# Output projection of two block pairs as seven products of sums in an attention and gated feed-forward kernel

## The chip, the cores and the metric

The kernel runs on one core of one Trainium2 chip. The metric is the device time of one execution in microseconds (us). The engines named below are TensorE (PE in the profile; its weight loads are PEld), VectorE (DVE), ScalarE (ACT), GpSimd (POOL) and SyncE (SP, which issues nearly all DMAs). TensorE, VectorE and ScalarE each carry out their instructions in the order in which the code emits them.

## The reference

Attention inside chunks of 64 positions, then a gated feed-forward layer over all tokens, in float32:

```
q_c, k_c, v_c: (8, 8, 9, 64, 64)        # batch, head, chunk, position, depth
attn = softmax(q_c @ k_c^T / 8)          # 64 x 64 per chunk and head
x = (attn @ v_c), as 4608 tokens x 512
g = x @ w_gate                           # 512 -> 1536
h = silu(g) * (x @ w_val)
out = h @ w_out                          # 1536 -> 512
```

## The kernel before

The 4608 tokens are nine blocks (`NB`) of 512 tokens (`N`); a block has four tiles (`T`) of 128 tokens. The 1536 inner columns are twelve steps (`NF`) of 128. Float32 accuracy comes from splitting each operand into a rounded high part and a low part (`split`, L60 to L63: a copy on ScalarE, a subtraction on VectorE) and adding three matmuls, low by high, high by low, high by high. Every matmul has its own weight load.

Blocks 0 to 2 run first. Blocks 3 to 8 run as three pairs, (3, 4), (5, 6) and (7, 8), here called pair 3, 5 and 7, in the loop at L1306. For a pair the gate and value products of both blocks come from seven products in place of eight (a scheme of Strassen's kind): `gated_pair` (L1152) calls `seventh` seven times per step, each six matmuls of 128x512 into PSUM (L883), and copies, adds and multiplies the results on ScalarE and VectorE (L1165 to L1189, `add` at L887, `times` at L522). Products 0, 2, 4 and 6 add up in one bank `ps1`, which is read between them. Its result is `h` for the first block and `h2` for the second.

The output projection is then done block by block. `project` (L537) multiplies the split `h` of one step (`hh`, `hl`, from `parts`, L529) by 512 columns of `w_out`, four tiles by three matmuls of 128x512 (L552 to L554), into the four banks of `ps_o`. For the first block of a pair this happens one step late inside `gated_pair`: `turn_of(t)` puts tile t's three matmuls between the products of the next step. The second block's `h2` is kept in SBUF (`both_steps`, L1200), and `second_steps` (L1211) projects it afterwards, twelve steps of twelve matmuls. The weights of a step, `both`, are fetched by `out_again` (L494) and the factors of the seven products by `load_weights` (L1144), both on SP's queue.

Beside a pair's steps run the scores, softmax and turned columns of the next pair's attention: `bursts` are short runs of small matmuls at the end of a step, `middle` and `behind` hold ScalarE and VectorE work, of which `turn_some` issues four 32x32 block transposes for each of its parts (L355). In pair 3 and pair 5 the sums and splits of the next pair's input (`x0`, `s1`, `x1`, `s4`, `s2`, `x2` to `x6`, L1104 to L1139) are made one per step of `second_steps`, from the list `later` (L1318). Step 11 of the last pair splits `h` ahead of its last product (`ending`, L1175), and the last tile of the last block is done in two column halves (L545 to L575).

PSUM has eight banks: two `ps_a`, two `ps_gv`, four `ps_o`. SBUF buffers are reused by tags, among them `moved(i)`, one of twelve large buffers.

## Time and profile before

| what | value |
|---|---|
| median of 3 runs | 891.84 us (891.74 to 892.16) |
| the profiled execution | 892.38 us |
| its span | 890.6 us |
| steps of pair 5, gated part | 515.57 to 671.50 us |
| second block of pair 5 | 671.5 to 704.3 us |
| steps of pair 7, gated part | 704.3 to 851.2 us |
| VectorE busy over the span | 547.6 us |
| ScalarE busy over the span | 389.0 us |
| DMA, mean | 251 GB/s |

Everything in the profile belongs to one execution, whose time is in the second line; its span is the part in which instructions ran. A row of the timeline gives the start and the duration in us, the engine, the line of the kernel, the operation, and output <- input with their shapes; in brackets stands how long the engine had been idle and what released it. A row of the groups ends in the total busy time, the mean of one in ns, and the idle time ahead. A row of the windows gives a stretch of the span, its length, the busy time of PE, PEld, DVE, ACT and POOL in it, the granted clock, and the DMA's share and GB/s. Matmuls are pipelined: the distance between two starts is what one costs, not its listed duration.

### The profile page before, as it was taken

To read this page: it belongs to the slowest core of one execution; us is meant where nothing else is said; L and a number is where in the kernel's file an instruction comes from. 1 tells how busy PE (TensorE), PEld (TensorE's weight loads), DVE (VectorE), ACT (ScalarE), POOL (GpSimd) and SP (SyncE) were. 2 spreads that over 40 slices of the span, in tenths; PEclk is the share of its full clock that TensorE was granted. 3 is DMA by queue.
4 is the path that set the end of the run, shared out by engine and by line. 5 is a ranking of instruction groups with operands and counts; after the bars stand their busy time and mean duration, and the time that the engine had idled before them with its cause. 6 is when DMAs were issued, how large, how long until landed. Compare 5 with 4: busy or idle time off the path is not lost.

```text
span 890.6 us, 14742 instructions
## 1 busy us (share of the span) xinstructions
PE 880.2 (99%) x6034; PEld 729.3 (82%) x6034; DVE 547.6 (61%) x831; ACT 389.0 (44%) x594; POOL 39.7 (4%) x32
## 2 busy tenths in 40 slices
PE   7999999999999999999999999999999999999998
PEld 6788888888888888888888888888888888888886
DVE  6888999673888656776753656767645433333332
ACT  5757777544442345225325444244325432223232
POOL 1100000000055110000000000000000000000000
PEclk9999999999999999999999999999999999999999
DMA  9767778889799777657577867566657475555651
GB/s 357 266 253 297 262 286 320 336 284 348 222 392 279 277 254 238 248 215 255 207 250 291 299 208 268 194 236 245 199 213 278 177 272 203 198 196 230 237 189 47
DMA packets 73314, 223.25 MB, mean 251 GB/s; under 512 B 30752, under 2 KB 31264, under 8 KB 59040
## 3 DMA queue, kind: packets, MB, share of 16 engines
q1 hardware_dynamic: 71664, 219.57, 67.7%
q10 hardware_dynamic: 1584, 2.75, 0.9%
q8 instruction: 47, 0.77, 0.3%
q14 instruction: 19, 0.16, 0.1%
HBM read 178.78 MB, written 43.52 MB: 250 GB/s over the span
## 4 chain that ended last, share of the span: by engine, by line
PE 94%; DVE 3%; DMA 1%; issue 1%; ACT 0%; SPq 0%; ACTq 0%; DVEq 0%
PE ps_a L883 26%; PE ps_gv L883 19%; PE ps_gv L478 12%; PE ps_o L552 11%; PE ps_o L553 11%; PE ps_o L554 11%; PE ps_a L290 2%; DMA qk_t<-in_qk 1%; PE ps_a L368 1%; PE ps_a L468 0%; DVE both L677 0%; DVE t L90 0%; DVE th L165 0%; DVE w L130 0%; DVE h L522 0%
## 5 line engine op out<-in xcount | busy, mean ns | idle before, releaser
L883 PE MATMUL ps_a<-x,factors 128*128 128x512 f32 x864 | 219.2, 389 | 0.0
L883 PEld LDWEIGHTS ps_a<-x,factors 128*128 128x128 f32 x864 | 162.2, 188 | 33.7
L883 PE MATMUL ps_gv<-x,factors 128*128 128x512 f32 x648 | 164.4, 389 | 0.0
L883 PEld LDWEIGHTS ps_gv<-x,factors 128*128 128x128 f32 x648 | 121.6, 188 | 25.3
L552 PE MATMUL ps_o<-both,hl 128*128 128x512 f32 x336 | 131.8, 392 | 0.0
L553 PE MATMUL ps_o<-both,hh 128*128 128x512 f32 x336 | 130.7, 389 | 0.0
L554 PE MATMUL ps_o<-both,hh 128*128 128x512 f32 x336 | 130.6, 389 | 0.0
L63 DVE TENSOR_TENSOR hl<-h,hh 128x512 fp32r<-128x512 f32 x98 | 68.2, 696 | 65.0 <-ACT hh L62 64.8
L62 ACT CAST hh<-h 128x512 fp32r<-128x512 f32 x98 | 60.5, 617 | 95.7 <-PE ps_o L554 51.3
L478 PE MATMUL ps_gv<-xh,w 128*128 128x512 f32 x320 | 97.9, 391 | 0.2 <-ACT xh L638 0.2
L887 DVE TENSOR_TENSOR h<-h,ps_gv 128x512 f32<-128x512 f32 x44 | 30.2, 686 | 103.9 <-PE ps_gv L883 103.7
L355 DVE STREAM_TRANSPOSE turned<-s_sb 32x256 f32<-32x256 f32 x192 | 83.7, 436 | 2.7
L522 DVE SCALAR_TENSOR_TENSOR h<-v,h 128x512 f32<-128x512 f32 x88 | 60.9, 692 | 38.0 <-ACT h L1188 33.3
L552 PEld LDWEIGHTS ps_o<-both,hl 128*128 128x128 f32 x336 | 63.0, 188 | 13.5
L554 PEld LDWEIGHTS ps_o<-both,hh 128*128 128x128 f32 x336 | 63.1, 188 | 13.2
L553 PEld LDWEIGHTS ps_o<-both,hh 128*128 128x128 f32 x336 | 63.1, 188 | 12.7
L1188 ACT ACTIVATE h<-ps_a 128x512 f32<-128x512 f32 x36 | 21.5, 598 | 112.2 <-PE ps_a L883 112.2
L478 PEld LDWEIGHTS ps_gv<-xh,w 128*128 128x128 f32 x320 | 59.8, 188 | 12.9 <-ACT xh L638 0.5
L478 PE MATMUL ps_gv<-xl,w 128*128 128x512 f32 x160 | 61.3, 393 | 0.0
L887 DVE TENSOR_TENSOR v<-v,ps_a 128x512 f32<-128x512 f32 x44 | 30.2, 687 | 41.1 <-PE ps_a L883 36.4
L1174 ACT ACTIVATE h<-h 128x512 f32<-128x512 f32 x36 | 22.8, 632 | 53.0 <-DVE h L887 52.9
L887 DVE TENSOR_TENSOR v<-v,ps_gv 128x512 f32<-128x512 f32 x44 | 30.2, 687 | 24.3 <-PE ps_gv L883 24.2
(143 smaller groups left out, 1069.0 us busy)
## 6 DMA issues: line engine op xcount, KB each, us to landing
factors<-w SPq DMA_DIRECT2D x36, 1024.0 KB, 4.8
factors<-t SPq DMA_DIRECT2D x36, 1024.0 KB, 6.0
both<-o SPq DMA_DIRECT2D x70, 512.0 KB, 6.4
w<-w SPq DMA_DIRECT2D x16, 1024.0 KB, 7.9
t<-th SPq DMA_DIRECT2D x24, 512.0 KB, 4.2
two<-o SPq DMA_DIRECT2D x12, 1024.0 KB, 5.2
raw<-in_wgv SPq DMA_DIRECT2D x11, 1024.0 KB, 8.6
qk_t<-in_qk SPq DMA_DIRECT2D x10, 1024.0 KB, 7.8
```

Source lines behind the costliest of these rows:

```text
L62: nc.scalar.copy(out=hi, in_=src)
L63: (engine or nc.vector).tensor_tensor(out=lo, in0=src, in1=hi.bitcast(F32), op=ALU.subtract)
L355: nc.vector.transpose(out=self.turned[to:to + 32, p:p + 2, j, :, 32 * (i % 2):32 * (i % 2) + 32], in_=src[32 * i:32 * i + 32, :, o // 2, 3 ...
L478: nc.tensor.matmul(ps, w, x, start=first and (k, i) == which[0], stop=last and (k, i) == which[-1])
L522: nc.vector.scalar_tensor_tensor(out=h, in0=pv, scalar=2.0 ** -8, in1=h, op0=ALU.mult, op1=ALU.mult)
L552: nc.tensor.matmul(to, hl[:, ts], woh[:, m], start=first, stop=False, skip_group_check=skip)
L553: nc.tensor.matmul(to, hh[:, ts], wol[:, m], start=False, stop=False, skip_group_check=skip)
L554: nc.tensor.matmul(to, hh[:, ts], woh[:, m], start=False, stop=f in (a.steps[1], a.steps[1] - final), skip_group_check=skip)
L883: nc.tensor.matmul(ps, w[u][:, k], x[i][v][:, k], start=first and k == 0 and n == 0, stop=k == NK // 2 - 1 and n == 2, skip_group_check=True)
L887: nc.vector.tensor_tensor(out=t, in0=t, in1=ps, op=ALU.add)
L1174: nc.scalar.activation(h, h, AF.Silu, scale=2.0 ** -8)
L1188: nc.scalar.activation(h2, ps1, AF.Silu, scale=2.0 ** -8)
```

## The change

For pairs 5 and 7 the output projection of both blocks together is also done by seven products. The matrix of `h` is cut into four: first or second block by even or odd steps. `w_out` is cut into four: even or odd steps by left or right half of the columns (`HM` = 256). Two of the seven products use `h` of the first block as it is, with the left half of the columns (`Left`); they are done inside the gated steps. The five others use sums (`s1_of` to `s4_of` of the operands `h`, and sums of `w_out`) and stand behind the gated steps, in `seven_products`, as 15 units of two steps each.

The sums of `w_out` are made once, in pair 3's `both_steps` by `out_sums`: additions on GpSimd, a rounding copy on ScalarE, five DMAs to DRAM for every two steps. `Seven.load_sums` fetches them again. `gated_seven` is `gated_pair` with `h` and `h2` kept for both blocks (`row`) and with all of the output matmuls in one place, ahead of product 6 (in burst steps behind it). `second_steps` is used for pair 3 alone. The next pair's attention moves to bursts in steps 1, 5, 8 and 10; its `x0` to `x6` are made in `seven_products`. The two-half ending of the last tile leaves `project`; `seven_products` ends with its own division by tiles.

```diff
@@ project @@
+        if hasattr(parts, "project"):
+            parts.project(which)
+            return
...
-            if ends:
-                more = ps_a.tile([P, DM // 2], F32, name="ps_a", tag="ps_a")
...
@@ gated_pair: the branch "ending" (split of h ahead of product 6) goes @@
@@ new @@
+    def out_sums(f, engine=nc.gpsimd):
+        if f % 2 == 0:
+            last_both[0] = out_now[f]
+            return
...
+        for i, w in enumerate((even, odd)):
+            w = w.bitcast(F32).rearrange("p j (c m) -> p j c m", c=2)
+            engine.tensor_tensor(out=t[:, i::2], in0=w[:, 0], in1=w[:, 1], op=ALU.add)
+        engine.tensor_tensor(out=sums[:, 0:2], in0=t[:, 2:4], in1=t[:, 0:3:2], op=ALU.subtract)
+        engine.tensor_tensor(out=sums[:, 2], in0=t[:, 3], in1=sums[:, 0], op=ALU.subtract)
+        engine.tensor_tensor(out=sums[:, 3], in0=t[:, 1], in1=sums[:, 2], op=ALU.subtract)
+        nc.scalar.copy(out=th, in_=sums)
+        engine.tensor_tensor(out=tl, in0=sums, in1=t, op=ALU.subtract)
...
+        nc.sync.dma_start(out=of_j[:, 2], in_=odd[:, :, HM:].bitcast(F32))
+        for h, src in enumerate((t, sums)):
+            nc.sync.dma_start(out=of_j[:, 0:2, h], in_=src[:, 0:3:2])
+            nc.sync.dma_start(out=of_j[:, 3:5, h], in_=src[:, 1:4:2])
+    class Left:
...
+        def project(self, which):
...
+            for t in which:
+                eighth(c.banks[self.f % 2][t // 2][:, t % 2], self.hh, self.hl, self.w, t,
+                       self.f < 2 and t % 2 == 0)
+    def eighth(to, hi, lo, w, t, first, last=True):
+        ts = slice(t * P, (t + 1) * P)
+        for n, (a, i) in enumerate(((lo, 0), (hi, 1), (hi, 0))):
+            nc.tensor.matmul(to, a[:, ts], w[:, i], start=first and n == 0, stop=last and n == 2, skip_group_check=True)
+    class Seven(Pair):
...
+        def s3(self, j):
+            self.combine(self.rows[0, 0, j], self.rows[0, 0, j], self.rows[1, 0, j], ALU.subtract)
+        def s1_of(self, j):
+            self.combine(self.rows[1, 0, j], self.rows[1, 0, j], self.rows[1, 1, j], ALU.add)
+        def s2_of(self, j):
...
+            self.combine(to, self.rows[1, 1, j], self.rows[0, 0, j], ALU.subtract)
+        def s4_of(self, j):
+            self.combine(self.rows[0, 1, j], self.rows[0, 1, j], self.rows[2, 0, j], ALU.subtract)
+        def split(self, k):
+            src = self.rows[((1, 0), (2, 0), (0, 1), (0, 0), (1, 1))[k // 3] + (k % 3,)]
...
+            split(src, *self.parts[k])
+        def unit(self, ps, k, first=False, tiles=range(T)):
+            hi, lo = self.parts[k]
+            for j in range(2):
+                u = 2 * k + j
+                for t in tiles:
+                    eighth(ps(t), hi[:, j], lo[:, j], self.w[u // 4][:, u % 4], t, first and j == 0 and (t % 2 == 0 or t == tiles[0]))
+        def finish(self, c, ps):
+            nc.vector.scalar_tensor_tensor(out=c, in0=ps, scalar=2.0 ** -8, in1=c, op0=ALU.mult, op1=ALU.add)
+        def snapshot(self, c, ps):
+            nc.scalar.activation(c, ps, AF.Copy, scale=2.0 ** -8)
+    def gated_seven(pair, f, burst, middle):
...
+        seventh(ps1, pair.x, loaded[f], 4, False)
+        add(v2, ps1)
+        seventh(ps2, pair.x, loaded[f], 5, False)
+        add(v1, ps2)
+        times(h, v1)
+        if not burst:
+            turns(range(T))
+        seventh(ps1, pair.x, loaded[f], 6, False)
+        nc.scalar.activation(h2, ps1, AF.Silu, scale=2.0 ** -8)
+        times(h2, v2)
+    def gated_steps(pair, middle, behind, bursts, nothing=lambda: None):
+        for f in range(NF):
+            w = hp.tile([P, 2, HM], F32R, name="left", tag=("h", "o_sb")[f % 2])
+            nc.sync.dma_start(out=w.bitcast(F32), in_=two_o[f // 2][:, f % 2, :, :HM])
+            gated_seven(pair, f, f in bursts, middle.get(f, nothing))
+            left = Left(pair, f, pair.row(0, f), w)
+            if f in bursts:
+                turns([0, 1])
+                bursts[f]()
+                turns([2, 3])
+            if f % 4 == 2:
+                pair.s3(f // 4)
+            if f % 4 == 3:
+                pair.s1_of(f // 4)
+            behind.get(f, nothing)()
+            pending.append((left, None))
...
+                pair.split(0)
+            else:
...
+                pair.split(1)
+    def seven_products(pair, n):
...
+        turns(range(T))
+        ps1, ps3 = pair.banks[0], pair.banks[1]
...
+        for c, ps in zip(c11, ps1):
+            pair.snapshot(c, ps)
...
+        def before_unit(k):
+            if k == 0:
+                pair.split(2)
+                pair.s2_of(0)
+                pair.split(3)
+                for u, c in enumerate(c11):
+                    pair.finish(c, ps3[u])
+                    pair.store(c, 0, 0, 2 * u)
+            elif k < 3:
+                pair.s2_of(k)
+                pair.split(k + 3)
+            elif k < 6:
+                pair.s4_of(k - 3)
+                pair.split(k + 3)
+            elif k < 11:
+                pair.split(k + 3)
...
+            if k == 3:
+                for u in range(2):
+                    pair.snapshot(c22[:, u], ps2[u])
...
+            if n:
+                for what in {3: (n.x0, n.s1), 4: (n.x1,), 5: (n.s4,), 6: (n.s2, n.x2), 11: (n.x3,),
+                             12: (n.x4, n.s5), 13: (n.x6,)}.get(k, ()):
+                    what()
...
+        for k in range(3 * 4):
+            before_unit(k)
+            pair.unit(lambda t: banks[k // 3][t // 2][:, t % 2], k, k == 0)
...
+        for tiles, ps, c in (((0, 1), last[0], c21[0]), ((2,), last[1][:, 0], c21[1][:, 0]), ((3,), last[2], c21[1][:, 1])):
+            for k in range(12, 15):
+                pair.unit(lambda t: ps[:, t % 2] if len(tiles) > 1 else ps, k, k == 12, tiles)
...
@@ loop over pairs: b == 3 as before, with out_sums(f) in both_steps; else @@
+                bursts = {1: lambda: scores(c), 5: lambda: scores(n.second()), 8: lambda: cross(c), 10: lambda: cross(n.a[1])}
+                middle = {2: lambda: c.exponents(0, NP), 6: lambda: n.a[1].exponents(0, NP)}
+                behind = {2: lambda: c.normalize(0, NP), 3: lambda: turn_some(c, 0, 3), 4: lambda: turn_some(c, 3, 3),
+                          5: lambda: turn_some(c, 6, 2), 6: lambda: (n.a[1].normalize(0, NP), load_values(c)),
+                          7: lambda: turn_some(n.a[1], 0, 3), 8: lambda: (turn_some(n.a[1], 3, 3), load_values(n.a[1])),
+                          9: lambda: turn_some(n.a[1], 6, 2)}
+            gated_steps(pair, middle, behind, bursts)
+            seven_products(pair, n)
```

More of the change, by code (lines that the diff above doesn't have):

```diff
@@ L496, in out_again @@
         recent[:] = [nc.sync.dma_start(out=both.bitcast(F32), in_=kept_o[f]).ins]
+        out_now[f] = both
         return both[:, 0], both[:, 1]
@@ L542, in project @@
             ts, o = slice(t * P, (t + 1) * P), a.o[t]
[L543 to L557 removed]
+            nc.tensor.matmul(o, hl[:, ts], woh, start=f == a.steps[0], stop=False)
+            nc.tensor.matmul(o, hh[:, ts], wol, start=False, stop=False)
+            nc.tensor.matmul(o, hh[:, ts], woh, start=False, stop=f == a.steps[1])
             if f == a.steps[1]:
@@ L561, in project @@
                 r = a.b * N + t * P
[L563 to L575 removed]
+                pool, tag = pools[t % 2]
+                o_sb = pool.tile([P, DM], F32, name="o_sb", tag=tag)
+                nc.scalar.activation(o_sb, o, AF.Copy, scale=2.0 ** -8)
+                nc.sync.dma_start(out=out[r:r + P, :], in_=o_sb)
     pending = []
@@ L1174, in gated_pair @@
         nc.scalar.activation(h, h, AF.Silu, scale=2.0 ** -8)
-        ending = pair.last and f == NF - 1
-        if not ending:
-            turn_of(1)
+        turn_of(1)
         seventh(ps1, pair.x, loaded[f], 4, False)
@@ new lines, in attn_then_gated_ffn, with __init__ @@
+    class Left:
+        def __init__(self, pair, f, h, w):
+            self.pair, self.f, self.w = pair, f, w
+            _, _, self.hh, self.hl = parts(None, f, h)
+        def project(self, which):
+            c = self.pair
+            if not c.banks:
+                for i in (1, 0):
+                    c.banks[i] = [ps_o.tile([P, 2, HM], F32, name="ps_o") for _ in range(2)]
+            for t in which:
+                eighth(c.banks[self.f % 2][t // 2][:, t % 2], self.hh, self.hl, self.w, t,
+                       self.f < 2 and t % 2 == 0)
@@ new lines, in gated_seven @@
+    def gated_seven(pair, f, burst, middle):
+        ps1 = ps_a.tile([P, N], F32, name="ps_a", tag="ps_a")
+        ps2 = ps_gv.tile([P, N], F32, name="ps_gv")
+        ps3 = ps_gv.tile([P, N], F32, name="ps_gv")
+        h, h2 = pair.row(0, f), pair.row(1, f)
+        v12 = const.tile([P, 2, N], F32, name="v", tag=("ts", "wo1")[f % 2])
+        v1, v2 = v12[:, 0], v12[:, 1]
+        seventh(ps1, pair.x, loaded[f], 0, True)
+        nc.scalar.copy(out=h, in_=ps1)
+        seventh(ps2, pair.x, loaded[f], 1, True)
+        nc.scalar.copy(out=v2, in_=ps2)
+        seventh(ps1, pair.x, loaded[f], 2, False)
+        nc.scalar.copy(out=v1, in_=ps1)
+        middle()
+        seventh(ps3, pair.x, loaded[f], 3, True)
+        add(h, ps3)
+        nc.scalar.activation(h, h, AF.Silu, scale=2.0 ** -8)
+        seventh(ps1, pair.x, loaded[f], 4, False)
[8 more added lines that the diff above has]
+        times(h2, v2)
@@ L1206, in both_steps @@
             pending.append((p, wo_f))
+            out_sums(f)
             if f + 2 < NF:
@@ L1226, in second_steps @@
             behind.get(f, nothing)()
-            if not pair.last and f in (4, 8):
+            if f in (4, 8):
                 load_weights(f // 8)
@@ L1306, in attn_then_gated_ffn @@
     for b in range(3, NB, 2):
-        pair.last = b + 2 == NB
-        middle, behind, bursts, later = {}, {}, {}, {}
-        if not pair.last:
-            n = Pair(b + 2, moved(11))
+        n, middle, behind, bursts = None, {}, {}, {}
+        if b + 2 < NB:
+            n = Seven(b + 2, moved(11))
             c = n.a[0]
+        if b == 3:
             bursts = {0: lambda: scores(c), 5: lambda: scores(n.second()), 8: lambda: cross(c), 11: lambda: cross(n.a[1])}
@@ L1318, in attn_then_gated_ffn @@
             later = dict(enumerate((n.x0, n.s1, n.x1, n.s4, n.s2, n.x2, n.x3, n.x4, n.s5, n.x5, n.x6)))
-        both_steps(pair, middle, behind, bursts)
-        second_steps(pair, later)
-        if not pair.last:
-            pair = n
-    lag(None, None)
+            both_steps(pair, middle, behind, bursts)
+            second_steps(pair, later)
+        else:
+            if n:
+                bursts = {1: lambda: scores(c), 5: lambda: scores(n.second()), 8: lambda: cross(c), 10: lambda: cross(n.a[1])}
[6 more added lines that the diff above has]
+            seven_products(pair, n)
+        pair = n
 def kernel(**inputs):
```

128 lines of the change are left out of this document (97 added, 31 removed).

## The prediction

> **What bounds the kernel now.** I read the page first: the busy times and the granted clock, then the chain that ended last, then the stretches of the two pairs that change.
>
> ```profile
> PE 880.2 (99%) x6034; PEld 729.3 (82%) x6034; DVE 547.6 (61%) x831; ACT 389.0 (44%) x594; POOL 39.7 (4%) x32
> PEclk9999999999999999999999999999999999999999
> PE 94%; DVE 3%; DMA 1%; issue 1%; ACT 0%; SPq 0%; ACTq 0%; DVEq 0%
> 515.57:671.50 155.93, 155.93 (x1161) 129.23 (x1160) 97.06 (x161) 59.50 (x94) 0.00 (x0) 1.00 0.64 226
> 704.30:851.20 146.90, 146.90 (x649) 121.63 (x649) 48.52 (x72) 44.23 (x76) 0.00 (x0) 1.00 0.57 213
> ```
>
> TensorE is the chain (94%) at full clock, and in the gated steps of pair 5 (first window) and of pair 7 (second) it never rests: 155.93 us busy of 155.93. So each matmul taken out there is time won, and each wait put in is time lost. VectorE has room on average (97 of 156 us), but the question will be where its work stands in its queue.
>
> **What the matmuls cost.** The timeline of the last output tile holds the only 256-wide matmuls; two copies of `h` one step apart give the 512-wide ones.
>
> ```profile
> 885.95 0.28 PE L552 MATMUL ps_o<-both,hl 128*128 128x256 f32 x1
> ...
> 886.07 0.28 PE L553 MATMUL ps_o<-both,hh 128*128 128x256 f32 x1
> 886.07 0.19 PEld L554 LDWEIGHTS ps_o<-both,hh 128*128 128x128 f32 x1
> ...
> 886.19 0.19 PEld L552 LDWEIGHTS ps_a<-both,hl 128*128 128x128 f32 x1
> ...
> 886.55 0.28 PE L554 MATMUL ps_a<-both,hh 128*128 128x256 f32 x1
> 730.46 0.59 ACT L1165 COPY h<-ps_a 128x512 f32<-128x512 f32 x1 [0.99 <-PE ps_a L883]
> 742.70 0.59 ACT L1165 COPY h<-ps_a 128x512 f32<-128x512 f32 x1 [0.99 <-PE ps_a L883]
> 202.26 1.75 PE pt L454 x16
> ```
>
> A step of 42 gated and 12 output matmuls takes 742.70 − 730.46 = 12.24 us, 0.2267 us each. The six half-width ones start 0.60/5 = 0.120 us apart, not 0.113. Their weight loads are listed at 0.19 us but start 0.12 apart too, and 16 transposes with one load each took 1.75 us, 0.109 each; so a load needs at most 0.109 and does not bind at 0.120.
>
> Per pair, 2 blocks × 12 steps × 12 = 288 matmuls (65.28 us) go. Seven products of 6 steps × 4 tiles × 3 = 504 half-width ones come: 144 inside the gated steps (`Left.project`), 360 behind them, 504 × 0.120 = 60.48 us. **Gain 4.8 us per pair, 9.6 in all.** An eighth of 65 us would be 8.2; the narrower matmul eats 3.4 of it.
>
> **The waits that come in.** (a) *Behind step 11.* The rows show the end of product 6 (617.46, where the next matmul starts) and what follows.
>
> ```profile
> 617.46 0.39 PE L552 MATMUL ps_o<-both,hl 128*128 128x512 f32 x1
> ...
> 617.65 0.60 ACT L1188 ACTIVATE h<-ps_a 128x512 f32<-128x512 f32 x1 [3.92 <-PE ps_a L883]
> ...
> 618.15 0.61 ACT L62 CAST hh<-h 128x512 fp32r<-128x512 f32 x1
> 618.28 0.69 DVE L522 SCALAR_TENSOR_TENSOR h<-v,h 128x512 f32<-128x512 f32 x1 [1.11 <-ACT h L1188]
> ...
> 618.89 0.68 DVE L63 TENSOR_TENSOR hl<-h,hh 128x512 fp32r<-128x512 f32 x1
> ...
> 619.50 5.37 DVE L355 STREAM_TRANSPOSE turned<-s_sb 32x256 f32<-32x256 f32 x12
> ...
> 624.90 0.69 DVE L887 TENSOR_TENSOR h<-h,ps_gv 128x512 f32<-128x512 f32 x1
> ...
> 625.88 0.69 DVE L887 TENSOR_TENSOR v<-v,ps_a 128x512 f32<-128x512 f32 x1 [0.29 <-PE ps_a L883]
> 104.45 0.68 DVE L887 TENSOR_TENSOR v<-v,ps_a 128x512 f32<-128x512 f32 x1
> 105.18 0.50 PE L883 MATMUL ps_a<-xl,th 128*128 128x512 f32 x1 [0.21 <-DVE v L887]
> 105.52 0.62 PE L883 MATMUL ps_a<-xh,th 128*128 128x512 f32 x2
> ```
>
> `hl` is done at 619.57, 2.1 us after product 6. Before, step 11 of pair 5 had a burst there, and the last pair split `h` ahead of product 6. In the new code `seven_products` begins with step 11's `Left.project`, whose first matmul needs `hl`, right behind product 6, and nothing lies between. A restart behind VectorE cost 0.05 us of handing over (105.13 to 105.18) and 0.11 more on the first matmul (0.34 instead of 0.23). So 2.1 + 0.16 = 2.3 us per pair, **4.6 in all**. VectorE and ScalarE are behind this wait, not the DMA; what is late next is part (c).
>
> (b) *In the gated steps of pair 5.* The output matmuls, formerly spread over a step, now stand in one lump ahead of product 6, or behind it in burst steps. Product 6 adds to the bank that `add(v2, ps1)` reads, so it waits for that. After 12 transposes VectorE did `add(h)` at 624.90 to 625.59 and `add(v2)` could have begun then: done by 626.2 (T + 8.75, with T = 617.46). Product 6 now stands at T + 6 × 1.36 = 8.16 in a burst step, at 9.60 in another (12 × 0.12 more). Burst step 5 (12 transposes ahead): 8.8 − 8.16 = 0.6 us. Step 4 and burst step 8 also have `s1_of` ahead (1.14 us, below): 9.94 − 9.60 = 0.3 and 9.94 − 8.16 = 1.8. **Sum 2.7 us**; all other steps come out at hundredths, and pair 7 has no attention beside it, so nothing.
>
> (c) *Behind the gated steps.* 15 units of 24 × 0.12 = 2.88 us each need a split operand of 128x1024: a ScalarE copy and a VectorE subtraction; splits 3 to 8 also need a combination first (`s2_of`, `s4_of`).
>
> ```profile
> 489.23 0.69 DVE L63 TENSOR_TENSOR hl<-h,hh 128x512 fp32r<-128x512 f32 x1
> 489.84 1.22 DVE L1109 TENSOR_TENSOR sum<-s_sb 128x1024 f32<-128x1024 f32 x1
> 498.00 1.22 DVE L1120 TENSOR_TENSOR s_sb<-sum,s_sb 128x1024 f32<-128x1024 f32 x1
> ...
> 499.98 1.05 ACT L62 CAST x<-s_sb 128x1024 fp32r<-128x1024 f32 x1
> 501.06 1.23 DVE L63 TENSOR_TENSOR x<-s_sb,x 128x1024 fp32r<-128x1024 f32 x1 [0.26 <-ACT x L62]
> ```
>
> A 1024-wide operation takes 1.22 on VectorE, 1.05 on ScalarE, 0.03 to hand over (501.03 to 501.06); an independent VectorE operation begins 0.08 before the last one's end (489.84 against 489.92), so adds 1.14, or 0.61 at 512. In units 0 to 5 the order is combine, copy, subtract, each needing the one before: 1.14 + 0.03 + 1.05 + 0.03 + 1.22 = **3.47 us against 2.88**. VectorE loses 0.6 per unit on TensorE, with a lead of three units.
>
> With zero at the end of product 6: `hl` 2.13, `s1_of(2)` 3.3, splits 1 and 2 at 4.4 and 5.6; then split 3 at 9.1, split 4 at 13.8 (two `finish` of 0.61 between), split 5 at 17.2, split 6 at 20.7. TensorE wants unit k at 3.7 + 2.88 k: unit 4 at 15.2, 5 at 18.1, 6 at 21.0. Just in time.
>
> In pair 7 split 7 is ready at 24.2 (wanted 23.9), split 8 at 27.6 (wanted 26.7), then no combinations are left: **1.0 us**.
>
> In pair 5 the next pair's operands stand in the same queue. Before unit 4's: `x0` (its copy queued behind two snapshots; done 22.7) and `s1` (23.8); so split 7 comes at 23.8 + 3.47 = 27.3. `x1` 28.4, split 8 at 31.9; `n.s4` 33.0, split 9 34.2; `n.s2` 35.3, its copy, `x2` 37.6, split 10 at 38.8. TensorE waits at unit 7 (23.9 to 27.3), at 8 (30.2 to 31.9) and at 10 (37.7 to 38.8): **6.4 us** with the restarts. From unit 11 on VectorE has caught up.
>
> (d) *Pair 3, `out_sums`.* GpSimd forms sums, ScalarE copies them in its queue, and six such rounds lie beside the steps.
>
> ```profile
> L148 POOL TENSOR_TENSOR th<-th 128x512 f32<-128x512 f32 x4 | 5.5, 1372 | 0.2
> L149 POOL TENSOR_TENSOR th<-th 128x256 f32<-128x256 f32 x4 | 5.2, 1296 | 0.3
> factors<-t SPq DMA_DIRECT2D x36, 1024.0 KB, 6.0
> both<-o SPq DMA_DIRECT2D x70, 512.0 KB, 6.4
> 716.60 1.52 PE L883 MATMUL ps_a<-x,factors 128*128 128x512 f32 x6
> ...
> 728.85 0.61 ACT L62 CAST hh<-h 128x512 fp32r<-128x512 f32 x1
> 729.03 0.32 SPq L496 DMA_DIRECT2D both<-o  x1
> 318.56 2.40 POOL L165 TENSOR_TENSOR th<-th 128x1024 fp32r<-128x1024 f32 x1 [22.28 <-ACT th L162]
> 319.46 2.58 DVE L63 TENSOR_TENSOR x<-s_sb,x 128x1024 fp32r<-128x1024 f32 x1 [1.21 <-ACT x L62]
> ```
>
> The odd `both` is asked for at the step's start and lands 6.4 later (6.6 into it). Two GpSimd operations at 1.37 and two at up to 1.30 bring 11.9; ScalarE reaches the copy behind `hh` at about 12.9 (728.85 + 0.61, step begun at 716.6). The copy's 1.05 us fill the gap before the next copy of `h` (730.46), with 1.2 us to spare until product 2. I take nothing: it lies beside matmuls. The cover is gone when GpSimd is over 2 us late; every us beyond costs six. The last sum (2.40) holds the SP queue to about 4.1 into the next step; 1 MB of weights, some 6 us to land, is wanted at 12.2: hidden, with under 2 us to spare. The other end of the bound is 6 us. Nothing can be gained here.
>
> VectorE's subtraction at 319.46 took 2.58 instead of 1.23 while GpSimd worked (318.56 to 320.96). [...]
>
> (e) *DMA and the end.* `left` (256 KB per step) is a quarter of what both block's weights took, the sums are 1 MB per two units and asked for at least four units (11.5 us) ahead of use; stores as before. The last tile ends with 256-wide matmuls, one VectorE operation and a store, as before. Taken at nothing, ±0.5.
>
> **Sum.** −9.6 + 4.6 + 2.7 + 6.4 + 1.0 = **+5.1 us**. The profiled execution took 892.38 (span 890.6), so 897.5; the median of the runs stands 0.54 lower, so **897.0 us**.
>
> **Rivals.** (1) *VectorE keeps up* (the other side). If its order lets splits run ahead, or units cost it under 2.88 us, (b) and (c) vanish and only (a) is left: −9.6 + 4.6 = −5.0, 886.8 us. The turning point is 5.0 us of (b) and (c) together, of which I count 10.1. For it: VectorE's busy share of 62% in pair 5's steps. Against it: 3.47 against 2.88 comes from measured rows. Chance 0.14; a middle course with half of these waits, 892, 0.09.
>
> (2) *GpSimd holds ScalarE* in pair 3: one us late beyond the cover in six rounds, +6, 903 us. [...] Chance 0.11.
>
> (3) *The clock falls.* TensorE would be idle 3.4 us ahead of unit 7, longer than anywhere behind the opening in this trace; were the next unit run at half clock, 2.88 us more, 900. PEclk shows 9 in all slices, so no row here has it. Chance 0.06. [...]
>
> (4) *Weight loads bind half-width matmuls* at their listed 0.19: 504 × 0.19 − 65.3 = +30 per pair, 951. The starts 0.12 apart speak against it: 0.02.
>
> The forecast itself has 0.58.
>
> **Chances and range.** A measurement of this kernel can tell about 0.2% (1.8 us) from no change. Faster: rival 1 and a third of the middle course, 0.17; same: most of the rest of it, 0.05, and the forecast's lower edge, 0.02; slower 0.76. The range reaches from 888 (part of the middle course) to 903 (GpSimd); it leaves out rival 1 and rival 4.
>
> **What would show it.** In the new trace: 256-wide starts 0.12 apart and 1008 of them; TensorE idle about 2.2 us behind each step 11, released by VectorE's `hl`; waits ahead of units 7, 8 and 10 of pair 5 released by splits, with VectorE busy nearly throughout; small waits of product 6 on `add(v2)` in steps 4, 5 and 8; no idle TensorE in pair 3's steps. I am wrong if splits are ready a unit ahead in pair 5, or if pair 3's steps are longer than 12.24 us.

## The result and the profile after

The changed kernel took **902.77 us** (median of 4 runs, 902.35 to 903.10) against 892.00 of the kernel before beside it (4 runs, 891.74 to 892.38): a ratio of 1.0118, 95% interval 1.0105 to 1.0130. It is slower by 10.8 us, twice the 5.1 that were forecast. The profiled execution took 902.35 us, with a span of 900.6; the one before had 892.38 and 890.6. The 10.0 us between these two are what the stages below have to add up to.

From the page of the changed kernel, the busy times, the granted clock and the chain that ended last:

```profile
PE 875.8 (97%) x6463; PEld 742.2 (82%) x6463; DVE 612.5 (68%) x875; ACT 409.8 (46%) x606; POOL 91.0 (10%) x68
PEclk9999999999999999999999999999999999999999
PE 82%; DVE 12%; ACT 3%; DMA 2%; issue 1%; SPq 0%; ACTq 0%; DVEq 0%
```

TensorE is busy 4.4 us less than before, at full clock; the time is lost while it stands. Its share of the chain fell from 94% to 82%, and VectorE's rose from 3% to 12%. The view of the waits names the places (engine, output and line that waited, what released it; us in total, times, the longest):

```profile
PE ps_gv L1216 <- DVE halves L63: 5.8, 4, 3.4
PE ps_o L1216 <- DVE hl L63: 4.0, 2, 2.0
PE ps_a L864 <- DVE v L868: 2.5, 4, 1.6
PE ps_o L545 <- DVE hl L63: 1.2, 2, 0.9
PE ps_o L1216 <- DVE halves L63: 0.9, 1, 0.9
PE ps_o L545 <- ACT o_sb L555: 0.8, 1, 0.8
```

The first and fifth line are part (c) of the prediction (units that wait for a split), the second part (a) (step 11's `hl`), the third part (b) (product 6 behind `add(v2)`; one of its four, 0.2 us early in the span, stands in the kernel before too). The fourth and sixth lie in pair 3's steps, part (d), for which nothing was counted.

How much each stage lost is read from the first matmul of a pair's gated steps, before:

```profile
515.58 1.30 PE L883 MATMUL ps_a<-x,factors 128*128 128x512 f32 x5
704.36 1.52 PE L883 MATMUL ps_a<-x,factors 128*128 128x512 f32 x6
```

and after:

```profile
518.53 1.30 PE L864 MATMUL ps_a<-x,factors 128*128 128x512 f32 x5
718.36 1.32 PE L864 MATMUL ps_a<-x,factors 128*128 128x512 f32 x5
```

Before, the last twelve output matmuls of pair 5 (2.72 us at 0.2267) stand in pair 7's first step; they are counted to pair 5 here.

| stretch | before | after | difference | forecast |
|---|---|---|---|---|
| up to pair 5's first product | 515.58 | 518.53 | **+2.95** | 0 |
| pair 5 | 188.78 + 2.72 | 199.83 | **+8.33** | +6.6 (−4.8 + 2.3 + 2.7 + 6.4) |
| pair 7 to the end of the span | 186.24 − 2.72 | 182.24 | **−1.28** | −1.5 (−4.8 + 2.3 + 1.0) |
| sum | | | +10.0 | +5.1 |

**Pair 5, behind the gated steps.** The timeline of TensorE there, step 11's `Left.project` first, then three units without a break, then the units with an idle time ahead:

```profile
666.90 0.39 PE L1216 MATMUL ps_o<-left,hl 128*128 128x256 f32 x1 [2.01 <-DVE hl L63]
...
668.44 8.80 PE L1216 MATMUL ps_gv<-sums,halves 128*128 128x256 f32 x72
...
692.30 3.13 PE L1216 MATMUL ps_gv<-sums,halves 128*128 128x256 f32 x24 [3.45 <-DVE halves L63]
696.99 3.13 PE L1216 MATMUL ps_gv<-sums,halves 128*128 128x256 f32 x24 [1.56 <-DVE halves L63]
703.87 14.66 PE L1216 MATMUL ps_o<-sums,halves 128*128 128x256 f32 x120 [0.87 <-DVE halves L63]
```

A half-width matmul costs (8.80 − 0.28) / 71 = 0.120 us. The waits stand at units 7, 8 and 10; counted from the end of product 6 (664.7, six matmuls of 0.227 us from 663.34), these units start at 27.6, 32.3 and 39.2 us, and the splits had been forecast for 27.3, 31.9 and 38.8.

**Pair 5, the gated steps.** The matmuls of product 6 that waited, in steps 4, 5 and 8 (counted from 0):

```profile
576.15 3.01 PE L864 MATMUL ps_a<-x,factors 128*128 128x512 f32 x12 [0.16 <-DVE v L868]
586.54 1.65 PE L864 MATMUL ps_a<-x,factors 128*128 128x512 f32 x6 [0.57 <-DVE v L868]
624.04 1.66 PE L864 MATMUL ps_a<-x,factors 128*128 128x512 f32 x6 [1.57 <-DVE v L868]
```

These are the three steps forecast, with 0.16, 0.57 and 1.57 us of idle time for 0.3, 0.6 and 1.8.

**Pair 3.** TensorE waits at three places, 0.86, 0.38 and 0.84 us, where it had no wait before. Two of them in the timeline, GpSimd's sums, VectorE's operations beside them and TensorE's matmul that waited:

```profile
364.52 2.71 POOL L1186 TENSOR_TENSOR ot<-both 128x512 f32<-128x512 f32 x2 [6.91 <-issue]
...
365.95 1.84 DVE L523 SCALAR_TENSOR_TENSOR h<-v,h 128x512 f32<-128x512 f32 x1 [1.12 <-ACT h L1164]
367.31 1.62 POOL L1187 TENSOR_TENSOR ot<-ot 128x512 f32<-128x512 f32 x1
...
367.71 1.77 DVE L63 TENSOR_TENSOR hl<-h,hh 128x512 fp32r<-128x512 f32 x1
...
369.54 0.50 PE L545 MATMUL ps_o<-both,hl 128*128 128x512 f32 x1 [0.86 <-DVE hl L63]
...
485.44 2.40 POOL L1191 TENSOR_TENSOR ot<-ot 128x1024 fp32r<-128x1024 f32 x1 [9.95 <-ACT ot L1190]
...
485.92 2.47 DVE L63 TENSOR_TENSOR hl<-h,hh 128x512 fp32r<-128x512 f32 x1 [3.39 <-ACT hh L62]
...
488.49 0.47 PE L545 MATMUL ps_o<-two,hl 128*128 128x512 f32 x1 [0.84 <-ACT o_sb L555]
```

The multiplication at 365.95 and the subtraction behind it took 1.84 and 1.77 us in place of 0.69 each. So `hl` was ready at 369.48. TensorE had wanted it at 368.68 (369.54 less 0.86), for tile 0 of the very next step. At 485.92 a subtraction of 0.69 took 2.47. Here the releaser named is ScalarE's copy `o_sb`, but `hl` was ready only at 488.39. The kernel without GpSimd's sums (below) speaks for `hl`: there the same matmul starts at 485.67 without a wait, in the middle of the same copies (483.94 to 486.46).

### The profile page after: what moved, and what is told of

It is laid out like the page before. It is cut to its first block, busy times and chain, and to the rows that moved or that the text cites. A ratio compares the mean times of both kernels' runs of the same rounds, so it can differ in the third digit from the quotient of the medians.

```text
span 900.6 us, 15752 instructions
## 1 busy us (share of the span) xinstructions
PE 875.8 (97%) x6463; PEld 742.2 (82%) x6463; DVE 612.5 (68%) x875; ACT 409.8 (46%) x606; POOL 91.0 (10%) x68
## 4 chain that ended last, share of the span: by engine, by line
PE 82%; DVE 12%; ACT 3%; DMA 2%; issue 1%; SPq 0%; ACTq 0%; DVEq 0%
PE ps_a L864 24%; PE ps_gv L864 17%; PE ps_gv L478 12%; PE ps_o L1216 7%; PE ps_o L545 6%; PE ps_o L546 6%; PE ps_o L547 6%; DVE halves L63 2%; PE ps_a L290 2%; DVE turned L355 2%; ACT halves L62 1%; DVE rows L1233 1%; DMA raw<-in_wgv 1%; PE ps_a L368 1%; DMA two<-o 1%
## 5 line engine op out<-in xcount | busy, mean ns | idle before, releaser
L545 PE MATMUL ps_o<-both,hl 128*128 128x512 f32 x208 | 81.9, 394 | 1.2 <-DVE hl L63 1.2
L546 PE MATMUL ps_o<-both,hh 128*128 128x512 f32 x208 | 81.0, 389 | 0.0
L547 PE MATMUL ps_o<-both,hh 128*128 128x512 f32 x208 | 81.0, 389 | 0.0
L63 DVE TENSOR_TENSOR hl<-h,hh 128x512 fp32r<-128x512 f32 x50 | 41.0, 820 | 29.1 <-ACT hh L62 29.1
L523 DVE SCALAR_TENSOR_TENSOR rows<-v,rows 128x512 f32<-128x512 f32 x48 | 33.2, 692 | 39.2 <-ACT rows L1305 35.7
L62 ACT CAST hh<-h 128x512 fp32r<-128x512 f32 x50 | 30.9, 618 | 58.2 <-DVE h L523 42.1
L1216 PE MATMUL ps_o<-sums,halves 128*128 128x256 f32 x414 | 50.6, 283 | 0.9 <-DVE halves L63 0.9
L868 DVE TENSOR_TENSOR rows<-rows,ps_gv 128x512 f32<-128x512 f32 x24 | 16.5, 688 | 51.1 <-PE ps_gv L864 45.2
L1216 PEld LDWEIGHTS ps_o<-sums,halves 128*128 128x128 f32 x414 | 50.0, 192 | 1.1 <-DVE halves L63 1.1
L545 PEld LDWEIGHTS ps_o<-both,hl 128*128 128x128 f32 x208 | 39.0, 188 | 10.3 <-DVE hl L63 2.1
L868 DVE TENSOR_TENSOR v<-v,ps_a 128x512 f32<-128x512 f32 x44 | 30.2, 685 | 24.1 <-ACT rows L1296 11.1
L547 PEld LDWEIGHTS ps_o<-both,hh 128*128 128x128 f32 x208 | 39.0, 188 | 8.2
L546 PEld LDWEIGHTS ps_o<-both,hh 128*128 128x128 f32 x208 | 39.1, 188 | 7.8
```

The source lines that it names most:

```text
L62: nc.scalar.copy(out=hi, in_=src)
L63: (engine or nc.vector).tensor_tensor(out=lo, in0=src, in1=hi.bitcast(F32), op=ALU.subtract)
L523: nc.vector.scalar_tensor_tensor(out=h, in0=pv, scalar=2.0 ** -8, in1=h, op0=ALU.mult, op1=ALU.mult)
L545: nc.tensor.matmul(o, hl[:, ts], woh, start=f == a.steps[0], stop=False)
L546: nc.tensor.matmul(o, hh[:, ts], wol, start=False, stop=False)
L547: nc.tensor.matmul(o, hh[:, ts], woh, start=False, stop=f == a.steps[1])
```

## The experiments

The theory after the result: four separate losses, (a) to (d), sit on the gain of 9.6 us, and each has its own cause in VectorE's queue or, for (d), in GpSimd's hold on it. The rival in each case is that the wait has another cause, or comes back behind the next wait. Ratios are to the kernel before, run on the same chip, with 95% intervals; "less" means against the changed kernel's 902.77 us.

**GpSimd's sums left out** (part d); raw halves of `w_out` are stored in their place:

```diff
-        for i, w in enumerate((even, odd)):
...
-        nc.scalar.copy(out=th, in_=sums)
-        engine.tensor_tensor(out=tl, in0=sums, in1=t, op=ALU.subtract)
+        raw = [w.bitcast(F32).rearrange("p j (c m) -> p (j c) m", c=2) for w in (even, odd)]
+        nc.scalar.copy(out=th, in_=raw[1])
```

> Leaves out the additions and subtractions that form the sums of w_out (raw halves are stored in their place); ScalarE's 128x1024 copy and the five DMAs of each round stay. Theory (GpSimd's additions beside VectorE's two-input operations make `hl` late in pair 3): pair 3's steps lose the 3.0 us that they gained, pair 5's first product starts at about 515.7 instead of 518.7, time about 899.8. Rival (ScalarE's copy in its queue, or the extra DMAs on SP's queue, hold the steps): start stays near 518.7, time about 902.8.

Measured 900.29 us, 1.0090 (1.0075 to 1.0105): 2.5 less. The groups of VectorE's instructions between 360 and 530 us (shape, count, busy us, mean ns, idle time ahead) show why, first of the changed kernel:

```profile
L63 DVE TENSOR_TENSOR hl<-h,hh 128x512 fp32r<-128x512 f32 x22 | 20.7, 942 | 11.4 <-ACT hh L62 11.4
L523 DVE SCALAR_TENSOR_TENSOR h<-v,h 128x512 f32<-128x512 f32 x20 | 17.9, 897 | 9.7 <-ACT h L1164 8.5 <-ACT h L1155 0.3
L868 DVE TENSOR_TENSOR v<-v,ps_a 128x512 f32<-128x512 f32 x11 | 7.6, 687 | 8.9 <-PE ps_a L864 6.2 <-ACT h L1155 2.0 <-ACT rows L1296 0.7
```

then of the kernel without GpSimd's sums:

```profile
L63 DVE TENSOR_TENSOR hl<-h,hh 128x512 fp32r<-128x512 f32 x22 | 15.2, 689 | 12.0 <-ACT hh L62 11.9
L523 DVE SCALAR_TENSOR_TENSOR h<-v,h 128x512 f32<-128x512 f32 x20 | 13.8, 692 | 10.2 <-ACT h L1164 9.0 <-ACT h L1155 0.3
```

The same 42 operations took 38.6 us with GpSimd beside them and 29.0 without: 9.6 us of VectorE, of which some 3 reached TensorE. The additions that read PSUM (L868) are not touched, 687 ns. ScalarE's copy and the DMAs stayed in this kernel; they alone cost nothing that can be seen, for pair 5's first product starts at 515.59 us here and at 515.58 in the kernel before.

**GpSimd's sums in shorter pieces** (part d, by another way):

```diff
-            engine.tensor_tensor(out=t[:, i::2], in0=w[:, 0], in1=w[:, 1], op=ALU.add)
-        engine.tensor_tensor(out=sums[:, 0:2], in0=t[:, 2:4], in1=t[:, 0:3:2], op=ALU.subtract)
+            for c in range(2):
+                engine.tensor_tensor(out=t[:, i + 2 * c], in0=w[:, 0, c], in1=w[:, 1, c], op=ALU.add)
+        for c in range(2):
+            engine.tensor_tensor(out=sums[:, c], in0=t[:, 2 + c], in1=t[:, 2 * c], op=ALU.subtract)
...
-        engine.tensor_tensor(out=tl, in0=sums, in1=t, op=ALU.subtract)
+        for c in range(4):
+            engine.tensor_tensor(out=tl[:, c], in0=sums[:, c], in1=t[:, c], op=ALU.subtract)
```

> GpSimd's additions and subtractions in out_sums are cut into pieces of half or a quarter of the length (128x256 in place of 128x512 and 128x1024); what is computed stays. Theory 1 (a two-input operation of VectorE that meets a GpSimd instruction stands until that instruction ends: 0.69 us became 1.84 beside L1186): it waits for a shorter instruction, the stretch falls from about 1.1 us to at most 0.6, and pair 3 loses about 1 us in place of 3.0: 901 us. Rival (the two engines share the passage at a rate, whatever the length of an instruction): the stretch stays, pair 3 still loses 3 us, and the time is 902.8 or a little more.

Measured 900.40 us, 1.0086 (1.0070 to 1.0103): 2.4 less, nearly all of what leaving the sums out brought, though GpSimd now works longer (48.7 us between 360 and 530, against 43.2). The same groups:

```profile
L63 DVE TENSOR_TENSOR hl<-h,hh 128x512 fp32r<-128x512 f32 x22 | 18.0, 817 | 11.9 <-ACT hh L62 11.8
L523 DVE SCALAR_TENSOR_TENSOR h<-v,h 128x512 f32<-128x512 f32 x20 | 15.3, 765 | 9.9 <-ACT h L1164 8.7 <-ACT h L1155 0.3
```

VectorE's stretch falls from 9.6 to 4.3 us, and what is left is mostly covered. How the two engines' instructions meet differs from run to run: the silu behind product 6 of pair 5's step 0 comes between 529.3 and 531.5 us in the seven kernels here with the long instructions (mean 530.3), and between 527.8 and 528.2 in the five with pieces or with none (the kernel with 64 transposes ahead of that step, at the end of this section, not counted). So part (d) costs 1.3 to 3.5 us from execution to execution, some 2.3 in the mean. The traces also show what ends the hold. In the changed kernel each of the twelve of these 42 operations that took 0.75 us or more ends 0.55 us behind the end of a GpSimd instruction (in the rows of pair 3 above, 367.79 behind 367.23, 369.48 behind 368.93, 488.39 behind 487.84), and so do those that are stretched in the kernel with pieces. That speaks against sharing at a rate and for a hold that lasts until GpSimd's instruction ends. The operations that are stretched have both inputs in SBUF; the five additions from PSUM (L868) that met a GpSimd instruction between 360 and 530 us of the changed kernel took 0.69 us, as the others did.

**Step 11's split ahead of product 6** (part a): `Left(pair, f, h, w)` of the last step is made ahead of product 6.

```diff
         times(h, v1)
+        left = Left(pair, f, h, w) if f == NF - 1 else None
         if not burst:
             turns(range(T))
...
         times(h2, v2)
+        return left or Left(pair, f, h, w)
```

> Step 11's split of h goes ahead of product 6 in pairs 5 and 7. Theory (behind it VectorE's chain of combination, copy and subtraction is the bound, 3.47 us per unit against 2.88, so a wait taken away at the front comes back at units 4 to 8): the waits for hl (2.0 us each) go, waits at units 4 to 8 grow by about 2.3 less 0.4 in each pair; saving only 0.4 us per pair, time about 902.0. Rival (the wait for hl is a cost of its own): saving 2.3 per pair, time about 898.2.

Measured 901.23 us, 1.0099 (1.0084 to 1.0114): 1.5 less, not 4.6, with an interval that overlaps the changed kernel's; so the traces have to tell. TensorE's timeline behind step 11 of pair 5 shows the wait go and come back:

```profile
664.33 0.39 PE L1216 MATMUL ps_o<-left,hl 128*128 128x256 f32 x1 [0.20 <-DVE hl L63]
680.92 3.14 PE L1216 MATMUL ps_o<-sums,halves 128*128 128x256 f32 x24 [0.41 <-DVE halves L63]
684.52 3.10 PE L1216 MATMUL ps_gv<-sums,halves 128*128 128x256 f32 x24 [0.46 <-ACT c L1278]
691.07 7.83 PE L1216 MATMUL ps_gv<-sums,halves 128*128 128x256 f32 x48 [3.46 <-DVE halves L63]
```

The 2.0 us ahead of the first matmul became 0.2, and the units, reached earlier, wait 0.4 and 0.5 us more at places that had had no wait. From step 11's silu behind product 6 to pair 7's first such silu it is 62.8 us in place of 63.3, and from pair 7's step 11 to the end 50.9 in place of 51.4: the split saves 0.5 us per pair, the 0.4 that were expected if VectorE's queue sets the end of this stretch; the rest of the 1.5 lies elsewhere (pair 5's steps began 1.1 us earlier here). The last row holds something else: 48 matmuls took 7.83 us, where 0.120 us each make 5.9. The view of the stretch behind the wait shows a granted clock of one half (0.50, ahead of the DMA's share):

```profile
691.60:695.01 3.41, 3.41 (x18) 3.41 (x18) 2.22 (x3) 1.61 (x2) 0.00 (x0) 0.50 0.00 0
```

It cost nothing here: the wait of 1.56 us that the changed kernel has behind its unit 7 is gone in its place, and from unit 7 to unit 10 it is 11.6 us in both.

**Operands one unit earlier** (part c): `s2_of` and `s4_of` of a unit are issued a unit earlier, so that VectorE combines the next operand while ScalarE copies this one.

```diff
+                pair.s2_of(1)
...
-            elif k < 3:
-                pair.s2_of(k)
-                pair.split(k + 3)
...
-                pair.s4_of(k - 3)
+                if k == 1:
+                    pair.s2_of(2)
+                elif k < 5:
+                    pair.s4_of(k - 2)
```

> The combinations s2_of and s4_of are made one unit earlier, so that ScalarE's copy of one split runs while VectorE does the next combination; same work. Theory (the round trip by ScalarE inside each unit makes the chain): VectorE needs 2.28 us per unit instead of 3.47, all waits for splits go in both pairs (6.7 us of PE idle in the new kernel), the waits for hl stay; time about 895.4. Rival (VectorE's total work in pair 5, 43 us beside 44.6, is the bound whatever the order): pair 7 saves 1.0, pair 5 keeps most of its 6.4; time about 900.

Measured 895.54 us, 1.0039 (1.0024 to 1.0053): 7.2 less, and all waits for `halves` are gone from the view of the waits, those of the next pair's operands too: once VectorE no longer waits for ScalarE within each unit, they fit. From split to split in the units it is 2.27 us, against 3.55 in the changed kernel. The profile holds another stretch at half clock, 1.3 us behind the 2.0 us wait for step 11's `hl`:

```profile
668.02:671.43 3.41, 3.41 (x19) 3.41 (x18) 3.41 (x4) 0.98 (x2) 0.00 (x0) 0.50 0.35 149
```

Sixteen matmuls start in these 3.41 us, which take 1.92 at 0.120 each, and with no wait left behind it the 1.5 us are lost. Four of the five runs have a mean granted clock of 0.998; the one at 1.0 took 893.82 us.

**Both of these together**:

> Both edits of the two kernels before. Theory: with VectorE's chain shortened, the early split of step 11 is worth what it was not worth alone: another 2 us per pair, time about 891.2. Rival (waits are independent): the sum of the two single savings, which by the theory's numbers would be about 894.6.

Measured 890.74 us (10 runs), 0.9982 (0.9972 to 0.9991): 12.0 less. Behind the earlier operands the split is worth 4.8 us (the ratio falls by 0.0057, with some 0.0017 to either side), but not by its wait alone. In the traces the stretch from step 11's silu behind product 6 to pair 7's first is 54.8 us, against 58.1 with the earlier operands alone and 63.3 in the changed kernel; from pair 7's step 11 to the end it is 48.1 against 49.9. So the split takes 1.8 us off in each pair, where alone it took 0.5, and with the wait the stretch at half clock goes, 1.5 us in pair 5: all ten runs have a granted clock of 0.999 or 1.0.

**Only the next pair's operands later** (part c, which half of it counts):

```diff
-                for what in {3: (n.x0, n.s1), 4: (n.x1,), 5: (n.s4,), 6: (n.s2, n.x2), 11: (n.x3,),
+                for what in {7: (n.x0, n.s1), 8: (n.x1,), 9: (n.s4,), 10: (n.s2, n.x2), 11: (n.x3,),
```

> Only the next pair's operands x0, s1, x1, s4, s2, x2 move from units 3 to 6 of pair 5's products to units 7 to 10; the splits stay behind their own copies. Theory (in pair 5 the queue is 6.4 us late because of these operands, in pair 7, which has none, 1.0): pair 5's units wait as pair 7's do, about 1 us in all, and the next pair's first products still find their operands: 897.4 us. Rival 1 (the chain combine, copy, subtract alone makes VectorE late): 902 us. Rival 2 (the operands are then late for pair 6's first products): the gain is given back there, 900 us or more.

Measured 898.03 us, 1.0066 (1.0051 to 1.0081): 4.7 less. TensorE's waits behind the first `hl`, to pair 7's first step:

```profile
688.72 3.13 PE L1216 MATMUL ps_gv<-sums,halves 128*128 128x256 f32 x24 [0.41 <-DVE halves L63]
692.28 3.13 PE L1216 MATMUL ps_gv<-sums,halves 128*128 128x256 f32 x24 [0.42 <-DVE halves L63]
716.90 1.67 PE L864 MATMUL ps_a<-x,factors 128*128 128x512 f32 x6 [1.46 <-ACT rows L1288]
```

With the restarts the units lose 1.1 us, the 1.0 forecast for a pair with nothing else in the queue; some 1.6 us are given back behind a copy in pair 7's first step. So both theories hold in part: these operands make 5.3 of the 6.4 us, and moved to the end they cost something there.

**The sums s3 and s1 later in the gated steps** (part b):

```diff
-            if f % 4 == 2:
-                pair.s3(f // 4)
-            if f % 4 == 3:
-                pair.s1_of(f // 4)
+            for what, j in {8: ((pair.s3, 0), (pair.s1_of, 0)), 10: ((pair.s3, 1), (pair.s1_of, 1), (pair.s3, 2)),
+                            11: ((pair.s1_of, 2),)}.get(f, ()):
+                what(j)
```

> VectorE's s3 and s1 of the later units leave gated steps 2 to 10 and stand in steps 8, 10 and 11. Theory (TensorE's waits for the sum v2 in steps 3, 4, 5 and 8 of the two gated phases come from these operations ahead of it in VectorE's queue): the waits of steps 3, 4, 7 and 8 fall, that of step 5 stays at about 0.6 us; pair 5 gains about 2 us: 900.8 us. Rival (the gated steps wait for ScalarE's copies or for the chain of additions itself, not for what is added to the queue): no gain, 902.8 us.

Measured 902.04 us (900.76 to 903.09), 1.0107 (1.0092 to 1.0122): 0.7 less, within the overlap of the intervals: a miss. The waits for `v2` did fall as expected (1.2 us in all for 2.5), but a new one stands in step 8's burst:

```profile
622.49 1.66 PE L864 MATMUL ps_a<-x,factors 128*128 128x512 f32 x6 [0.45 <-DVE v L868]
...
624.79 2.12 PE L368 MATMUL ps_a<-turned,v_t 64*64 64x64 f32 x128
...
627.07 0.28 PE L1216 MATMUL ps_o<-left,hh 128*128 128x256 f32 x1
628.91 0.28 PE L1216 MATMUL ps_o<-left,hh 128*128 128x256 f32 x1 [1.55 <-issue]
```

Product 6 waits 0.45 us there in place of 1.57, and then TensorE stands 1.55 us at a matmul whose operands its neighbours already use. The profile names no releaser.

**All four edits**, with the next pair's operands spread over units 6 to 13:

> Four edits together: the split of step 11 ahead of product 6, each unit's operands one unit earlier, the sums s3 and s1 later in the gated steps, and GpSimd's sums in pieces; the next pair's operands are spread over units 6 to 13. Theory (the losses are separate waits, and the smaller number of matmuls is worth 9.6 us): from 890.7 us with the first two, less 2 for the gated steps and 1 to 2 for GpSimd's pieces: 887 to 888 us, about 0.5% below the kernel before. Rival (a wait removed comes back behind the next one): 890 to 891 us.

Measured **887.45 us** (887.18 to 887.71), 0.9944 (0.9929 to 0.9959): faster than the kernel before (892.50 beside it) by 5.0 us. The stall is there again, 1.53 us at the same matmul.

**The same without the later sums**:

> The four edits without the later sums: s3 and s1 of the later units stand in gated steps 2 to 10 again. Theory 1 (VectorE's waits that the later sums remove in pair 5, some 2 us, came back as the stall of 1.5 us in step 8's burst): the sums' place is worth only 0.5 us: 887.9 us, with TensorE's 2.5 us of waits for v2 and no stall. Rival (the sums' place is worth its 2 us): 889.5 us.

Measured 888.24 us, 0.9953 (0.9939 to 0.9968): the later sums are worth only some 0.8 us here, and the intervals overlap. The stall in step 8's burst is not there, the waits for `v2` are (2.3 us): the one had taken the place of the other.

**A load held back.** The view of the DMAs in a window shows a packet of an instruction queue in flight just ahead of the stall (626.67 to 627.63 us in the trace of the later sums; the stall ends at 628.91). So the load of step 10's factors was written into the middle of step 9, alone and with all four edits:

```diff
+            if f == 9:
+                inside = lambda: (load_weights(10), middle.get(9, nothing)())
...
-                load_weights(f + 2)
+                if f != 8:
+                    load_weights(f + 2)
```

> The kernel with the later sums (s3, s1 in steps 8, 10 and 11), and besides the load of step 10's factors (2 MB) is issued in the middle of step 9 in place of the end of step 8. In the profile of the later sums alone TensorE stood 1.55 us in step 8's burst at a matmul for which nothing is named, and an instruction packet had been in flight shortly before, beside the factors. Theory (TensorE's own program comes in packets over the same DMA engines, the burst of 128 small matmuls uses one up in 2 us, and the next is late behind the factors): with the factors held back the stall goes, and what the later sums were meant to bring is seen: 900.5 us, against 902.0. Rival (the stall has to do with VectorE's two sums behind step 8 or comes by chance): it stays, 902 us.

> The four edits together, and the load of step 10's factors in the middle of step 9. Theory (the stall of 1.53 us in step 8's burst is the late packet of TensorE's program behind the factors): it goes, 885.9 us. Rival (it isn't): 887.4 us.

Measured 901.42 us, 1.0104 (1.0088 to 1.0121), and 887.33 us, 0.9943 (0.9928 to 0.9958), with stalls of 1.56 and 1.67 us. This tells nothing on the factors: in the traces the two halves of the load went out around step 8's product 6, as they had without the edit (in the trace of the later sums at 622.07 and 624.18 us, product 6 from 622.49). Both are repeats of the kernels they came from, and as such show the stall to be no accident: four profiled executions have it, with 1.53 to 1.67 us. The same place is idle for 0.05 to 0.31 us in the changed kernel and the seven other kernels above, also with no releaser named. In all twelve executions the matmul that ends the idle time, the third or fourth behind the 128 small ones, starts 1.28 to 1.48 us behind the end of such a packet. What differs is when the packet is in flight: it begins 0.3 to 0.5 us after the first small matmul in the eight, 1.8 to 1.9 after it in the four.

**TensorE's program shifted.** 64 small transposes ahead of pair 5's steps:

```diff
+        if bursts:
+            ps = ps_gv.tile([P, P], F32, name="unread", tag="ps_gv")
+            for _ in range(64):
+                nc.tensor.transpose(ps[:32, :32], ident[:32, :32], ident[:32, :32])
```

> The four edits together, with 64 small transposes (32x32, read by nobody) on TensorE ahead of pair 5's gated steps: everything behind them stands 64 matmuls and 64 weight loads later in TensorE's program. In four profiled executions TensorE stood 1.5 to 1.7 us in step 8's burst at one and the same matmul, the third behind the 128 small ones, for which no releaser is named; the queue of instruction packets shows 51 packets of 0.84 MB in all for 12926 matmuls and loads, so one for about 253 of them, as many as the 128 small ones with their loads are. The kernels that held the load of the factors back did not shift that load in the trace, so the question is still open. Theory (TensorE waits for the next packet of its own program): the stall moves by 64 matmuls to an earlier place, into the 128 small ones, and is about as long. Rival (the stall belongs to that matmul, its bank or its weights): it stays at the third matmul behind the small ones. The time is 888 to 889 us either way, 1 us for the transposes.

Measured 887.97 us, 0.9949 (0.9933 to 0.9966), with 2.0 us for the transposes themselves. Step 8's burst, in TensorE's timeline:

```profile
621.79 1.67 PE L864 MATMUL ps_a<-x,factors 128*128 128x512 f32 x6 [0.46 <-DVE v L868]
...
624.11 2.13 PE L368 MATMUL ps_a<-turned,v_t 64*64 64x64 f32 x128
626.16 0.38 PE L1219 MATMUL ps_o<-left,hl 128*128 128x256 f32 x1
626.38 0.40 PE L1219 MATMUL ps_o<-left,hh 128*128 128x256 f32 x2
```

The stall is gone, from this place and from all of pair 5. The stall hangs on the position in TensorE's program, not on that matmul, its bank or its weights, which are the same; by this one profiled execution that rival falls. But it did not move into the burst, as the theory had it. The trace shows why that need not follow: the last packet ahead of the burst is in flight from 608.01 to 608.94 us here, 15 us before the first small matmul, and the next from 628.33. With the stall gone, pair 5's gated steps (silu behind product 6, step 0 to step 11) take 131.7 us, against 133.9 in the kernel with the stall and in the changed kernel: the 2 us that the later sums were meant to bring.

## Why the prediction came out as it did

The direction, the mechanisms of (a), (b) and (c) and the places of their waits were right. The size was half of what came. Idle TensorE in pair 3's steps, which the prediction had named as a sign that it is wrong, is what the trace shows.

| term | forecast | measured | from |
|---|---|---|---|
| matmuls | −9.6 | −9.6 | 0.120 us each, as forecast |
| (a) step 11's `hl` | 4.6 | 4.3 | 2.01 + 0.16 for the restart, twice |
| (b) gated steps of pair 5 | 2.7 | 4.5 | what is left of pair 5's +8.33 |
| (c) pair 5 | 6.4 | 6.4 | 3.45 + 1.56 + 0.87 + three restarts |
| (c) pair 7 and the end | 1.0 | 1.3 | what is left of −1.28 |
| (d) pair 3 | 0 | 3.0 | first product of pair 5 |

- **The step that failed is (d).** The prediction had the hold of GpSimd on VectorE before it, with a row (2.58 us in place of 1.23), and counted nothing for it. Tile 0's `hl` is wanted near the start of the next step: in the row above without a hold it would have been there at 367.3 (the kernel without GpSimd's sums has it at 367.28), TensorE came at 368.68, so the cover was 1.4 us; two operations in a row were stretched by 1.15 and 1.08, one behind the other. I had counted the cover for GpSimd's and ScalarE's work, and none for VectorE's. Leaving the sums out took 2.5 us off, cutting them into pieces 2.4. This term and the shortfall of (b) make up nearly all of the 4.9 us between forecast and measurement.
- **(b) was right in its mechanism and too small.** From silu to silu (behind product 6), against 11.0 us (9.5 in a step with a burst, whose output matmuls stand behind product 6), steps 4, 5 and 8 lost 0.42, 0.87 and 1.89 us, 3.2 in all for the 2.7 forecast, since each short wait also pays the restart; and steps 3 and 7, "at hundredths", lost 0.3 each. Another 0.3 is the idle time behind step 8's burst (step 9 took 14.98 us, 14.68 in the shifted kernel); the rest of the 4.5 was not traced to a cause. The shifted kernel, in which s3 and s1 stand elsewhere and no stall takes their place, has its steps 3, 4 and 7 at 11.0 us: there these sums are the cause.
- **(c) and (a) were right to some tenths** (the chain per unit measured 3.55 us from split to split in pair 7, for 3.47), and the run with only the next pair's operands moved confirms the split of (c) into 5.3 us for them and 1.1 for the chain of combine, copy and subtract.
- **Rival 1** (VectorE keeps up) was not what happened, but with operands issued a unit earlier it does: 890.74 us with the early split, 888.24 with GpSimd's pieces and the next pair's operands spread besides. **Rival 2** met the time (903) by chance: pair 3 lost 3.0 us and not 6, and not ScalarE was held for a late copy, but VectorE's own operations were stretched. The range reached up to the measured time only by the price of that rival.
- **Rival 3** (the clock falls) did come, though not in the profiled execution of the changed kernel: there the clock stayed at 1.0 through an idle time of 3.45 us ahead of unit 7, and the unit's 24 matmuls took 3.13 us, as after shorter waits. Its three other runs have a mean granted clock of 0.996 to 0.998. In six of the twelve edited kernels the profiled execution has ten stretches of 3.41 us at half clock in all, each beginning at most 1.6 us behind the end of an idle time of 2.0 to 3.5 us; between the opening and the end none stands behind a shorter one, and not every idle time of that length has one. For the changed kernel it mattered little: the run at 1.0 took 902.35 us, the three others 902.58 to 903.10. Where VectorE's queue sets the time, a slower unit only shortens the next wait (ahead of unit 7 it is 2.1 us in place of 3.45 where the clock had fallen behind step 11's wait); that cover is missing in the rival's price of 2.88 us. No run shows that price either: a unit at half clock throughout would take 5.76 us, and the stretches were 3.41 long; the one behind step 11's wait in the kernel with earlier operands cost 1.5. **Rival 4** (weight loads) did not come: half-width matmuls cost 0.120 us.

## What to carry to other kernels

Work that is taken off a full engine and paid for with additions elsewhere is worth only what the queue of the other engine can follow; look at the chain per unit (here 3.55 us against 2.88), and put each operand's combination a unit ahead before counting the gain. When an idle engine is given work, ask whom it holds up: here two-input operations of VectorE on SBUF stood until GpSimd's instruction had ended (0.69 us became up to 1.84 beside 128x512), and the same sums in shorter GpSimd instructions took 2.4 us less in all. Removing one wait alone tells little of its worth: the early split shortened its stretch by 0.5 us per pair by itself and by 1.8 behind the second edit, and there it took a stretch at half clock away besides.

## What the runs showed of the hardware

- GpSimd's instructions stretched VectorE's operations with two inputs in SBUF from 0.69 to 1.84 us (beside 128x512) and to 2.47 (beside 128x1024), and left additions with one input in PSUM at 0.69. The stretched operations end 0.55 us behind the end of GpSimd's instruction.
- The granted clock of TensorE fell to one half for 3.41 us behind ten idle times of 2.0 to 3.5 us, in six profiled executions. Such a stretch cost 1.5 us where nothing else set the time, and nothing where TensorE went on to wait for VectorE.
- TensorE stood at a place that hangs on its own program, with no other engine named. The page lists a queue of instruction packets:

```profile
q8 instruction: 51, 0.84, 0.4%
```

51 packets and 0.84 MB for 12926 matmuls and weight loads would be one packet for some 253 of them (an estimate, if these packets bring TensorE's program), and the burst of 128 small matmuls with their loads is as many, run through in 2.1 us; twelve gated matmuls with their loads take 2.7 us. The stall of 1.5 to 1.7 us stood right behind such a burst, came where the wait ahead of the burst had become 1.1 us shorter, and went when the program was shifted by 128 instructions. The start of the matmul 1.28 to 1.48 us behind the packet's end, whether TensorE stood 0.05 or 1.67 us, speaks for a wait for that packet; what made the packet late was not settled, since the one edit meant to test the factors' part did not move their load.
